# Two token blocks by turns through the first five weight slices of layer 0, with partial sums put aside

## The chip, the cores and the metric

The kernel runs on one core of one Trainium2 chip. Five engines have instruction queues of their own: TensorE (PE in the profile, PEld its weight loads), VectorE (DVE), ScalarE (ACT), GpSimd (POOL) and SyncE (SP), which here only issues DMAs. The metric is the device time of one execution in microseconds. Before the change it is 1027.12 us, the median of three runs (1025.68 to 1028.23).

## The reference, cut to what matters

```python
# linear attention with a decay per channel: batch 4, 8 heads, 768 tokens, head size 48
for t in range(S):
    cur = u * k_t (outer) v_t
    y[:, :, t] = r_t @ (state + cur)
    state = w * state + k_t (outer) v_t
x = y.transpose(0, 2, 1, 3).reshape(3072, 384)
def layer(x, w_gate, w_val, w_out):           # 384 -> 1536 -> 384
    return silu(x @ w_gate) * (x @ w_val) @ w_out
x = layer(x, moe weights)
x = layer(x / rms(x) * rms_g, moe2 weights)   # rms over the 384 of one token
```

Weights, inputs and outputs are float64 on the caller's side. The kernel gets the doubles' bits, and reads r, k, v as it needs them.

## The kernel before, in words

The 3072 tokens are eight token blocks of 384 (one half of the sequence of one batch). A pass of one block through one layer is a pair J = (layer, block). The hidden size of 1536 is cut into twelve slices of 128 (f = 0 to 11). One step of the kernel is one slice of one pass: nine matmuls for the gate (`pg`), nine for the value (`pv`), both L852, then silu (ACT, `sl`, L974), the product (DVE, `sl`, L984), a split of the product into two f16 parts (ACT `hh` L988, POOL `hl` L992), and nine matmuls that add to the output sums (`po`, L862). The nine are three products of f16 parts, for three pieces each. The output sums of a pass stay in three PSUM banks po0 to po2 over all twelve steps. At the end of a pass `evacuate` (L878, L880) takes them out; for layer 0, squares, the inverse rms on POOL (L897 to L904), scaling and a transposition (L916) follow, and the block goes to DRAM until layer 1 takes it up.

The order of passes is `ORD`: (0,0), (0,1), (0,2), (1,0), (0,3), (1,1) and so on: layer 0 leads by three. Step t is slice t % 12 of pass t // 12, so block 0 of layer 0 has steps 0 to 11, block 1 steps 12 to 23, block 2 steps 24 to 35, and layer 1 begins at step 36.

Two other kinds of work run beside the steps.

Weights: each slice arrives as doubles (`raw`, DMAs L770 to L772), and is decoded: two passes on ACT that check magnitudes (`w_abs` L799, `w_check` L804), three on DVE that put the bits together (`w_bits`, L817, L819, L821), one on ACT for the high f16 part (`w_hi`, L838) and one on DVE for the low part (`w_lo`, L842). A step needs its slice decoded. The twelve slices of layer 0 are all decoded once and kept, then layer 1's.

Attention: a block's x comes from four units of two heads each. Block 0's four units (`Unit`) work with chunks of 128 tokens: k and r are loaded (L361) into `first`, transposed (L377), weighted with tables on DVE and POOL (G: L385, F: L388), multiplied on PE (L399 to L462), with a carried state (`st` L441, `carry` L446, `sbd` L451), and give `xh` (ACT L475) and `xl` (DVE L479). Units from 4 on work with chunks of 64: transposes and weighting on DVE (L666, L514), products on POOL (L528, L529, L537, L543), states `pd` (PE L682), the carried part (ACT L609), a scan (DVE L614), the scaled states `sb` (ACT L688), `pa` (PE L676, DVE L591), and `py` (PE L566). Unit n's `pd` comes after unit n-1's `py`. Units 4 to 7 make block 1, units 8 to 11 block 2. The tables for chunks of 64 are built on POOL by `split_tables` (L725 to L735), and units from 4 on wait for them, for the end of the first four units and for three buffers that POOL clears (L718).

The order of instructions in every engine's queue is fixed when the program is built. A planner (`Plan`) gets jobs with an engine, an estimated cost and what must come before; it walks through its own estimate of time, and each time gives the engine that is free first a job that is ready, that with the longest way to the end first among those ready within 0.3 us. An engine then does its jobs in that order, whatever their real times. `due` spreads the ends of a block's units over the steps ahead of its first step, as hints for that order. DMAs from SP are a queue of the same kind ("D").

Three lines carry the order of steps before:

```python
    at_step = {J: i * NF for i, J in enumerate(ORD)}
        J, f = ORD[t // NF], t % NF
            free = [("e",) + ORD[t // NF - 1] + (g,) for g in range(NG)]
```

Of the kernel before, what the change touches and what calls it, by code (L numbers as in the profile page):

```python
# [18 lines left out]
P = 128  # L19
# [5 lines left out]
AB = 7  # L25
# [10 lines left out]
LEAD = 3  # L36
C2 = 64
# [102 lines left out]
def fast_path(ctx, tc, r, k, v, w, u, wg1, wv1, wo1, wg2, wv2, wo2, rms_g, out):  # L140
# [193 lines left out]
    class Unit:  # L334
# [385 lines left out]
    def split_tables():  # L720

        g = nc.gpsimd
        for t, x, y, reps in ((F2, E, pw[:, :, 0:8], 1), (G2, iE, ipw, 2)):
            xs = l_tile([P, HP, 8], f"xs{reps}")
            g.tensor_scalar(out=xs, in0=x[:, :, 4:12], scalar1=2.0**AB, scalar2=None, op0=ALU.mult)  # L725
            for hp in range(HP):
                for i in range(reps):
                    g.tensor_mul(
                        t[:, hp, C2 * i : C2 * i + C2].rearrange("p (a b) -> p a b", b=8),
                        xs[:, hp].unsqueeze(2).to_broadcast([P, 8, 8]), y[:, hp].unsqueeze(1).to_broadcast([P, 8, 8]))  # L730
        for j in range(2):
# [3 lines left out]
        g.tensor_scalar(out=w_carry, in0=p2[:, 1], scalar1=2.0**AB, scalar2=None, op0=ALU.mult)  # L735
# [303 lines left out]
    xts, acc, post = {}, {}, {}  # L1039
# [7 lines left out]
    at_step = {J: i * NF for i, J in enumerate(ORD)}  # L1047
# [17 lines left out]
    def last(what, J):  # L1065
        return [(what, at_step[J] + NF - 1)] if J in at_step else []
# [12 lines left out]
    add("rmsg", "D", 0.5, [("lr", HP - 1)], setup_loads2)  # L1079
    add("bonus", "D", 0.95, [("lr", HP - 1)], setup_loads3)  # L1080
# [4 lines left out]
    add("ws0", "G", 0.4, ["c1"], lambda: nc.gpsimd.memset(wscan, 0.0))  # L1085
    add("wok", "V", 0.4, ["tables", ("xl", NU1 - 1)], decay_range)

    def due(j, i):

        if not j:  # L1090
            return []
        lo, hi = at_step[0, j - 1], at_step[0, j]
        return [("g", lo + (hi - lo) * (i + 1) // HP - 1)]


    for un in units[:NU1]:
# [20 lines left out]
        add(("cy", n), "A", 0.25, [("st", n), "tables2"], lambda un=un: un.hand_on())  # L1117
        add(("sbd", n), "A", 0.82, [("st", n), "c1"] + prior("y", 2), lambda un=un: un.states2())
# [10 lines left out]
    add("tables2", "G", 4.5, ["tables", "c1"], split_tables)  # L1129
# [3 lines left out]
    for un in units[NU1:NU2]:  # L1133
# [7 lines left out]
        job_("lk", "D", 1.8, [("lr", NU1 - 1)] + p("tk", 2) + p("lr"), lambda un=un: un.load(0))  # L1141
# [76 lines left out]
    def w_jobs(q, scale, wcost, ready, ahead):  # L1218
# [4 lines left out]
        add(("abs",) + q, "A", 0.19 + 0.96 * scale, [("w",) + q] + step("chk", prev) + (held(q) if q[0] else []), lambda: w_abs(q))  # L1223
# [4 lines left out]
        add(("hi",) + q, "A", 0.19 + 0.9 * scale, [("b", 3) + q] + ([("chk",) + q] if q[0] else held(q)), lambda: w_hi(q))  # L1228
# [13 lines left out]
    def held(q):  # L1242

        tag = f"{'uv'[q[0]]}{q[1] // 2}"
        return [x for p_ in lay if RAW_AT[p_[0]][p_[1]] == tag and (p_ < q[:2] or not q[0]) for x in used(p_)]

    seq = lay + [(1, f, n) for f in range(NWH, NF) for n in "gvo"]
    for i, q in enumerate(seq):
# [4 lines left out]
        ready = [("lr", HP - 1)] + ([("w", 0, NF - 1)] if q[0] else [])  # L1253
# [8 lines left out]
    for j in range(NBLK):  # L1262
        add(("lx", j), "D", 2.1, [("put", j), ("chk", 0, NF - 1)] + ([("xl2", j - 1), ("vl2", j - 1)] if j else []),
# [15 lines left out]
    for t in range(2 * NT):  # L1279
        J, f = ORD[t // NF], t % NF  # L1280
# [198 lines left out]
```

## Time and profile before

| | |
|---|---|
| median of the runs | 1027.12 us (1025.68 to 1028.23) |
| the profiled execution | 1029.09 us, its span 1027.4 us |
| mean granted TensorE clock | 0.976 |
| PE busy | 980.6 us (95%), 7903 matmuls |
| DVE busy | 523.4 us (51%) |
| ACT busy | 519.5 us (51%) |
| POOL busy | 436.8 us (43%) |
| DMA | 76.87 MB, mean 75 GB/s |

Shares over the whole span mix a beginning, in which all engines and the DMA work at once, with a long stretch in which PE is busy nearly all of the time. How an engine stands in one stretch is read from the lines by slices and from tables of stretches. In the timeline a row has the start, the length, the engine, the code line, the operation, tiles and shapes, the count, and in brackets the idle time ahead of it with what ended it.

### The profile page before, as it was taken

The numbers are of one execution on the slowest core, as the hardware profiler recorded it, in microseconds if no ns is written. First come the engines' busy times: TensorE is split into PE (matmuls) and PEld (weight loads), VectorE is DVE, ScalarE is ACT, GpSimd is POOL, SyncE is SP. The second block draws the span as 40 slices with busy tenths as digits, with TensorE's granted clock in tenths as the row PEclk, the third lists the DMA queues.
The fourth block names the chain that finished last, engine by engine and source line by source line (L and its number), as shares of the span: only waits on it lengthen the run. The fifth ranks groups of instructions, "written<-read, shape, count | busy, mean of one in ns | idle before, by whom it ended". The sixth has DMA issues, their size and how long they took to land.

```text
span 1027.4 us, 19923 instructions
## 1 busy us (share of the span) xinstructions
PE 980.6 (95%) x7903; PEld 612.8 (60%) x7903; DVE 523.4 (51%) x817; ACT 519.5 (51%) x1121; POOL 436.8 (43%) x489
## 2 busy tenths in 40 slices
PE   6887898989999999999999999999999999999996
PEld 3655665646666666666666666666666666666663
DVE  6889997997634434474443534464332412131211
ACT  1987755865644745474455635465453524342322
POOL 9255474444353435544455335544343223321121
PEclk7889998999999999999999999999999999999998
DMA  7988765647441312331122311321010100200000
GB/s 179 226 217 208 219 185 121 169 125 125 108 47 35 84 41 46 58 94 42 33 34 51 83 41 41 64 60 41 2 24 2 54 1 3 53 24 1 24 1 27
DMA packets 152741, 76.87 MB, mean 75 GB/s; under 512 B 115648, under 2 KB 141248, under 8 KB 152640
## 3 DMA queue, kind: packets, MB, share of 16 engines
q1 hardware_dynamic: 152256, 74.93, 30.7%
q8 instruction: 64, 1.05, 0.5%
q0 software_dynamic: 384, 0.59, 0.3%
q14 instruction: 37, 0.30, 0.1%
HBM read 66.03 MB, written 9.45 MB: 73 GB/s over the span
## 4 chain that ended last, share of the span: by engine, by line
PE 70%; DVE 7%; POOL 6%; ACT 6%; issue 4%; DMA 4%; SPq 2%; DVEq 0%; POOLq 0%; ACTq 0%
PE pv L852 22%; PE pg L852 22%; PE po L862 22%; PE py L566 3%; ACT sb L630 2%; POOL hl L992 2%; POOL ap L524 2%; DMA raw<-in_moe_w_out_dram 1%; PE pd L577 1%; DVE st L614 1%; SPq L361 1%; DVE fi L819 1%; DVE fi L821 1%; ACT hh L988 1%; DVE w L842 1%
## 5 line engine op out<-in xcount | busy, mean ns | idle before, releaser
L852 PEld LDWEIGHTS <-w 128*128 128x128 f16 x3456 | 336.4, 99 | 237.4 <-issue 22.3
L992 POOL TENSOR_TENSOR hl<-sl,hh 128x384 f16<-128x384 f32 x191 | 188.2, 986 | 472.4 <-ACT hh L988 465.9
L862 PE MATMUL po<-w,hh 128*128 128x384 f16 x1152 | 282.8, 328 | 1.3 <-ACT xo L878 1.3
L988 ACT ACTIVATE hh<-sl 128x384 f16<-128x384 f32 x192 | 100.0, 521 | 339.9 <-DVE sl L982 194.8
L862 PE MATMUL po<-w,hl 128*128 128x384 f16 x576 | 189.0, 328 | 7.8 <-POOL hl L992 7.7
L982 DVE SCALAR_TENSOR_TENSOR sl<-sl,pv 128x384 f32<-128x384 f32 x96 | 53.1, 554 | 236.0 <-PE pv L852 203.0
L852 PE MATMUL pg<-xh,w 128*128 128x384 f16 x576 | 159.0, 331 | 12.1 <-DVE sl L984 9.6
L852 PE MATMUL pv<-xh,w 128*128 128x384 f16 x576 | 159.4, 332 | 0.0
L862 PEld LDWEIGHTS <-hh 128*128 128x128 f16 x1152 | 111.9, 98 | 74.4 <-issue 2.5
L852 PE MATMUL pv<-x2v,w 128*128 128x384 f16 x864 | 156.2, 326 | 0.0
L852 PE MATMUL pg<-x2g,w 128*128 128x384 f16 x864 | 156.1, 326 | 0.0
L984 DVE TENSOR_TENSOR sl<-sl,pv 128x384 f32<-128x384 f32 x96 | 52.7, 550 | 121.4 <-PE pv L852 117.3
L974 ACT ACTIVATE sl<-pg 128x384 f32<-128x384 f32 x192 | 93.3, 486 | 28.9 <-PE pg L852 27.9
L852 PE MATMUL pg<-xl,w 128*128 128x384 f16 x288 | 95.4, 331 | 1.3 <-DVE xl L479 1.3
L852 PE MATMUL pv<-xl,w 128*128 128x384 f16 x288 | 95.6, 332 | 0.0
L862 PEld LDWEIGHTS <-hl 128*128 128x128 f16 x576 | 56.6, 98 | 47.4 <-POOL hl L992 9.6
L614 DVE TENSOR_TENSOR_SCAN st<-wscan,pd 128x288 f32<-128x288 f32 x28 | 21.0, 750 | 45.6 <-ACT pd L609 26.1
L566 PE MATMUL py<-rp,sb 128*128 128x64 f16 (+1 forms) x400 | 39.3, 212 | 0.4 <-ACT sb L688 0.4
L842 DVE SCALAR_TENSOR_TENSOR w<-fi,w 128x1152 f16<-128x1152 f32 (+1 forms) x30 | 36.6, 1229 | 1.3 <-ACT w L838 1.3
L838 ACT ACTIVATE w<-fi 128x1152 f16<-128x1152 f32 (+1 forms) x30 | 28.8, 963 | 13.0 <-DVE fi L821 12.9
L475 ACT ACTIVATE xh<-py 96x384 f16<-96x384 f32 (+1 forms) x42 | 20.2, 482 | 27.9 <-PE py L566 27.6
L819 DVE SCALAR_TENSOR_TENSOR fi<-raw,fi 128x1152 int32<-128x1152 int32 x21 | 32.4, 1544 | 0.4
(209 smaller groups left out, 1190.2 us busy)
## 6 DMA issues: line engine op xcount, KB each, us to landing
raw<-in_moe_w_out_dram SPq DMA_DIRECT2D x21, 384.0 KB, 5.4
kts<-in_k_dram SPq DMA_DIRECT2D x112, 70.0 KB, 2.8
rts<-in_r_dram SPq DMA_DIRECT2D x112, 70.0 KB, 2.0
xs_d<-tt SPq DMA_DIRECT2D x32, 144.0 KB, 3.8
xt<-xs_d SPq DMA_DIRECT2D x32, 144.0 KB, 3.1
nk<-in_k_dram SPq DMA_DIRECT2D x56, 72.0 KB, 2.7
nr<-in_r_dram SPq DMA_DIRECT2D x56, 72.0 KB, 2.5
out_dram<-xo SPq DMA_DIRECT2D x7, 576.0 KB, 2.9
```

Source lines behind the costliest of these rows:

```text
L566: nc.tensor.matmul(out, a, x, start=i == 0, stop=i == len(pairs) - 1)
L614: nc.vector.tensor_tensor_scan(st, wscan, self.pd, 0.0, ALU.mult, ALU.add)
L819: vec.scalar_tensor_tensor(out=fis[q], in0=high, scalar=-0x40000000, in1=fis[q], op0=ALU.bitwise_and, op1=ALU.bitwise_or)
L838: nc.scalar.activation(out=w_parts(q)[0], in_=fis[q].bitcast(F32), func=AF.Copy, scale=2.0**WS)
L842: nc.vector.scalar_tensor_tensor(out=lo, in0=fis.pop(q).bitcast(F32), scalar=2.0**WS, in1=hi, op0=ALU.mult, op1=ALU.subtract)
L852: nc.tensor.matmul(pt, a[:, kt, :], x[:, kt, :], start=i == 0, stop=i == last)
L862: nc.tensor.matmul(po[g], a[:, sl], x, start=f == 0 and i == 0, stop=f == NF - 1 and i == 2)
L974: nc.scalar.activation(out=sl, in_=job[t]["g"], func=AF.Silu, scale=2.0 ** -(WS + (X2S if J[0] else X1S)))
L982: nc.vector.scalar_tensor_tensor(out=sl, in0=sl, scalar=2.0 ** (H2S - WS - V2S), in1=job[t]["v"], op0=ALU.mult, op1=ALU.mult)
L984: nc.vector.tensor_mul(sl, sl, job[t]["v"])
L988: nc.scalar.activation(out=job[t]["h"][0], in_=job[t]["sl"], func=AF.Copy)
L992: (nc.vector if t == 2 * NT - 1 else nc.gpsimd).tensor_sub(hl, job[t]["sl"], hh)
```

## The change

Six things are changed. The names are those of the planner's jobs.

1. Passes (0,0) and (0,1) are each cut in two at slice 5 (`CUT`). The steps are: slices 0 to 4 of block 0 (steps 0 to 4), slices 0 to 4 of block 1 (5 to 9), slices 5 to 11 of block 0 (10 to 16), slices 5 to 11 of block 1 (17 to 23). From step 24 on the order is as before. Block 1's x is due from step 5 on, block 2's spread over steps 17 to 24.
2. After slice 4 of each, `put_aside` takes the three output sums out of PSUM into an SBUF tile (one on DVE, two on ACT); at the end of the pass DVE adds it to the second part's sums (three `scalar_tensor_tensor` in place of an ACT or DVE copy).
3. The loads of r of the first four units are issued by ScalarE's queue, those of k by SyncE's. The weights' loads wait for the last k only.
4. `tables2` (`split_tables`) and the clearing of `wscan` come after the last product of the first four units on POOL. Its last line, `w_carry`, becomes a job of DVE.
5. `carry` and `sbd` of the first four units are made by DVE, not ACT.
6. The magnitudes of layer 0's weights are kept where the high part goes, not in a buffer of their own; so `w_hi` waits for `w_check`. The buffers "xt" and "tt" hold the partial sums meanwhile. The first load of a layer 1 block waits for the evacuation of block 1.

```diff
+CUT = 5
-        def load_rows(self, t, src):
+        def load_rows(self, t, src, eng=nc.sync):
...
-                    nc.sync.dma_start(out=t[q : q + 32, 0:RUN],
+                    eng.dma_start(out=t[q : q + 32, 0:RUN],
...
-            nc.scalar.activation(out=carry[self.hp], in_=self.st[:, NC], func=AF.Copy, scale=w_carry[:, self.hp : self.hp + 1])
+            nc.vector.tensor_scalar(out=carry[self.hp], in0=self.st[:, NC], scalar1=w_carry[:, self.hp : self.hp + 1], scalar2=None,
+                                    op0=ALU.mult)
...
-                nc.scalar.activation(out=sbd[self.par][q, :, D * j : D * j + D], in_=self.st[q, 0:NC], func=AF.Copy,
-                                     scale=w128(self.hp)[q])
+                nc.vector.tensor_scalar(out=sbd[self.par][q, :, D * j : D * j + D], in0=self.st[q, 0:NC], scalar1=w128(self.hp)[q],
+                                        scalar2=None, op0=ALU.mult)
...
+        mags[q] = w_parts(q)[0].bitcast(BF16)
...
+    def put_aside(J, g):
+        if J not in aside:
+            aside[J] = xi.tile([P, NG, DM], F32, tag=("tt", "xt")[J[1]], name="aside")
+        scale = 2.0 ** -(X1S + 2 * WS)
+        if g:
+            nc.scalar.activation(out=aside[J][:, g], in_=acc[J][g], func=AF.Copy, scale=scale)
+        else:
+            nc.vector.tensor_scalar(out=aside[J][:, g], in0=acc[J][g], scalar1=scale, scalar2=None, op0=ALU.mult)
...
+        if J in aside:
+            nc.vector.scalar_tensor_tensor(out=xo, in0=po, scalar=scale, in1=aside[J][:, g], op0=ALU.mult, op1=ALU.add)
...
+    SEG = [((0, j), *fs) for fs in ((0, CUT), (CUT, NF)) for j in range(2)] + [(J, 0, NF) for J in ORD[2:]]
+    STEPS = [(J, f) for J, f0, f1 in SEG for f in range(f0, f1)]
+    at_step = {J: STEPS.index((J, 0)) for J in ORD}
+    end_step = {J: STEPS.index((J, NF - 1)) for J in ORD}
...
-        lo, hi = at_step[0, j - 1], at_step[0, j]
+        lo, hi = max(at_step[0, j - 1], end_step[0, j - 2] + 1 if j > 1 else 0), at_step[0, j]
...
-        add(("lr", n), "D", 1.8, [("lk", n)], lambda un=un: un.load(1))
+        add(("lr", n), "A", 1.8, [("at", n)] + ([("lr", i - 1)] if i else ["table"]), lambda un=un: un.load(1, nc.scalar), lat=4.0)
...
-    add("tables2", "G", 4.5, ["tables", "c1"], split_tables)
+    add("w_carry", "V", 0.1, ["tables"], carry_scale)
+    add("tables2", "G", 4.5, ["tables", "c1", ("rk", HP - 1)], split_tables)
...
-        add(("hi",) + q, "A", 0.19 + 0.9 * scale, [("b", 3) + q] + ([("chk",) + q] if q[0] else held(q)), lambda: w_hi(q))
+        add(("hi",) + q, "A", 0.19 + 0.9 * scale, [("b", 3) + q, ("chk",) + q], lambda: w_hi(q))
...
-        if f:
+        if f > f0:
             free = [("o", t - 1)]
         elif t:
-            free = [("e",) + ORD[t // NF - 1] + (g,) for g in range(NG)]
+            free = [(("e" if SEG[at - 1][2] == NF else "pe"),) + SEG[at - 1][0] + (g,) for g in range(NG)]
...
+    for J, f0, f1 in SEG:
+        if f1 < NF:
+            for g in range(NG):
+                add(("pe",) + J + (g,), "A" if g else "V", 0.58, [("o", STEPS.index((J, f1 - 1)))], lambda J=J, g=g: put_aside(J, g))
```

## Rows read from the trace of the kernel before

**Rows 1.** The page: PE's busy tenths in 40 slices of the span

```profile
PE   6887898989999999999999999999999999999996
```

**Rows 2.** Stretches: length, busy us of PE, PEld, DVE, ACT, POOL, clock, DMA share, GB/s

```profile
46.37:134.73 88.36, 74.14 (x603) 47.46 (x603) 81.00 (x94) 66.70 (x108) 45.55 (x36) 0.90 0.81 218
134.73:208.84 74.11, 70.08 (x582) 45.16 (x580) 67.51 (x79) 49.65 (x91) 42.09 (x41) 0.95 0.60 150
```

**Rows 3.** PE's timeline: first gate matmuls of steps 12, 24, 36 and 39

```profile
134.73 0.33 PE L852 MATMUL pg<-xh,w 128*128 128x384 f16 x1
...
208.84 0.33 PE L852 MATMUL pg<-xh,w 128*128 128x384 f16 x1
...
274.36 0.81 PE L852 MATMUL pg<-x2g,w 128*128 128x384 f16 x4
...
287.52 0.65 PE L852 MATMUL pg<-x2g,w 128*128 128x384 f16 x3
```

**Rows 4.** Groups by line, 46.37 to 134.73 us: busy us, mean ns, idle before

```profile
L842 DVE SCALAR_TENSOR_TENSOR w<-fi,w 128x1152 f16<-128x1152 f32 x11 | 17.1, 1554 | 1.3 <-ACT w L838 1.3
...
L819 DVE SCALAR_TENSOR_TENSOR fi<-raw,fi 128x1152 int32<-128x1152 int32 x9 | 14.7, 1638 | 0.1
L821 DVE SCALAR_TENSOR_TENSOR fi<-raw,fi 128x1152 int32<-128x1152 int32 x10 | 14.1, 1408 | 0.0
...
L817 DVE TENSOR_SCALAR fi<-raw 128x1152 int32<-128x1152 int32 x9 | 7.3, 808 | 0.0
...
L984 DVE TENSOR_TENSOR sl<-sl,pv 128x384 f32<-128x384 f32 x11 | 5.9, 541 | 0.0
```

**Rows 5.** PE's timeline: py of units 4, 5 and 6, and pd of unit 5

```profile
73.55 0.30 PE L566 MATMUL py<-af,vb 128*96 128x64 f32 x2
...
75.66 0.79 PE L682 MATMUL pd<-nv,ep 64*64 64x48 f32 x20
...
80.92 0.30 PE L566 MATMUL py<-ap,nv 128*96 128x64 f32 x2
...
105.50 0.30 PE L566 MATMUL py<-af,vb 128*96 128x64 f32 x2
```

**Rows 6.** Timelines of DVE and ACT: unit 5's scan and states, unit 7's x

```profile
76.76 0.74 DVE L614 TENSOR_TENSOR_SCAN st<-wscan,pd 128x288 f32<-128x288 f32 x1
...
77.53 1.67 ACT L688 ACTIVATE sb<-st,p 64x288 f32<-64x288 f32 x2 [0.83 <-DVE st L614]
...
124.19 1.47 ACT L475 ACTIVATE xh<-py 32x384 f16<-32x384 f32 x3
...
126.66 1.69 DVE L479 SCALAR_TENSOR_TENSOR xl<-py,xh 32x384 f16<-32x384 f32 x3
```

**Rows 7.** Timelines of DVE, POOL and PE: around the first product with F

```profile
10.95 0.38 DVE L306 TENSOR_TENSOR F<-E,pw 128x128 f32<-128x128 f32 x1
...
10.19 0.31 POOL L725 TENSOR_SCALAR xs<-E 128x32 f32<-128x32 f32 x1
...
15.68 1.00 POOL L388 TENSOR_TENSOR first<-first,F 128x384 f32<-128x384 f32 x1
...
16.73 2.24 PE L420 MATMUL att<-first 64*128 64x128 f32 x12 [7.78 <-POOL first L388]
```

**Rows 8.** SP's timeline: first load of weights; then two stretches

```profile
17.64 0.42 SPq L770 DMA_DIRECT2D raw<-in_moe_w_gate_dram x1
...
10.00:20.00 10.00, 3.27 (x18) 3.04 (x18) 9.50 (x19) 0.00 (x0) 9.53 (x27) 0.64 0.72 174
20.00:30.00 10.00, 9.41 (x70) 7.20 (x70) 4.44 (x14) 6.37 (x19) 6.01 (x7) 0.67 0.99 240
```

**Rows 9.** PE's timeline: three waits, the last at step 7

```profile
157.13 0.50 PE L862 MATMUL po<-w,hl 128*128 128x384 f16 x1 [3.56 <-POOL hl L992]
...
220.55 0.48 PE L862 MATMUL po<-w,hh 128*128 128x384 f16 x2 [1.25 <-ACT xo L878]
...
100.89 0.32 PE L852 MATMUL pg<-xh,w 128*128 128x384 f16 x1 [3.00 <-DVE sl L984]
```

More of the change, by code (lines that the diff above doesn't have):

```diff
@@ L854, in in_mm, with out_mm @@
         return pt
-    def out_mm(h, w_, f, po):
+    def out_mm(h, w_, po, first, last):
         hh, hl = h
@@ L861, in out_mm @@
             for i, (a, x) in enumerate(((hh, wh), (hh, wl), (hl, wh))):
-                nc.tensor.matmul(po[g], a[:, sl], x, start=f == 0 and i == 0, stop=f == NF - 1 and i == 2)
+                nc.tensor.matmul(po[g], a[:, sl], x, start=first and i == 0, stop=last and i == 2)
     def on_act(layer, blk):
-        return () if (layer, blk) == (1, NBLK - 1) else (1,) if layer else (0, 1)
+        return () if (layer, blk) in ((0, 0), (0, 1), (1, NBLK - 1)) else (1,) if layer else (0, 1)
+    def put_aside(J, g):
[6 more added lines that the diff above has]
+            nc.vector.tensor_scalar(out=aside[J][:, g], in0=acc[J][g], scalar1=scale, scalar2=None, op0=ALU.mult)
     def evacuate(layer, blk, g):
@@ L992, in step_hl, with step_o @@
         (nc.vector if t == 2 * NT - 1 else nc.gpsimd).tensor_sub(hl, job[t]["sl"], hh)
-    def step_o(t, f, q, J):
-        if f == 0:
+    def step_o(t, q, J, first, last):
+        if first:
             acc[J] = [ps.tile([P, DM], F32, tag=f"po{g}", name=f"po{g}") for g in range(NG)]
-        out_mm(job.pop(t)["h"], W[q + ("o",)], f, acc[J])
+        out_mm(job.pop(t)["h"], W[q + ("o",)], acc[J], first, last)
     def check_range():
@@ L1065, in last @@
     def last(what, J):
-        return [(what, at_step[J] + NF - 1)] if J in at_step else []
+        return [(what, end_step[J])] if J in end_step else []
     add("wu", "D", 1.9, [], load_tables)
@@ L1222, in w_jobs @@
         add(("w",) + q, "D", wcost, ready, (lambda: w_load(*q)) if len(q) == 2 else (lambda: w_load2(q[1], q[2])))
-        add(("abs",) + q, "A", 0.19 + 0.96 * scale, [("w",) + q] + step("chk", prev) + (held(q) if q[0] else []), lambda: w_abs(q))
+        add(("abs",) + q, "A", 0.19 + 0.96 * scale, [("w",) + q] + step("chk", prev) + held(q), lambda: w_abs(q))
         add(("chk",) + q, "A", 0.28 + 0.96 * scale, [("abs",) + q, "c1"], lambda: w_check(q))
@@ L1244, in held @@
         tag = f"{'uv'[q[0]]}{q[1] // 2}"
-        return [x for p_ in lay if RAW_AT[p_[0]][p_[1]] == tag and (p_ < q[:2] or not q[0]) for x in used(p_)]
+        return [x for p_ in lay if RAW_AT[p_[0]][p_[1]] == tag and p_ < q[:2] for x in used(p_)]
     seq = lay + [(1, f, n) for f in range(NWH, NF) for n in "gvo"]
@@ L1252, in fast_path @@
             continue
-        ready = [("lr", HP - 1)] + ([("w", 0, NF - 1)] if q[0] else [])
+        ready = [("lk", HP - 1)] + ([("w", 0, NF - 1)] if q[0] else [])
         tag = RAW_AT[q[0]][q[1]]
@@ L1262, in fast_path @@
     for j in range(NBLK):
-        add(("lx", j), "D", 2.1, [("put", j), ("chk", 0, NF - 1)] + ([("xl2", j - 1), ("vl2", j - 1)] if j else []),
+        add(("lx", j), "D", 2.1, [("put", j)] + [("e", 0, 1, g) for g in range(NG)] + ([("xl2", j - 1), ("vl2", j - 1)] if j else []),
             lambda j=j: post.__setitem__(("xt", j), load_x2(j)))
@@ L1279, in fast_path @@
     for t in range(2 * NT):
-        J, f = ORD[t // NF], t % NF
+        J, f = STEPS[t]
+        J0, f0, f1 = next(x for x in SEG if x[0] == J and x[1] <= f < x[2])
+        at = SEG.index((J0, f0, f1))
         layer, blk = J
```

37 lines of the change are left out of this document (17 added, 20 removed).

## The prediction

> **What bounds the kernel now.** I read the page's lines by slices first: PE is at nine tenths or more from the eighth slice of 25.7 us on, and not before [rows 1]. So time can be won only in the first 200 us or so, or by fewer matmuls, and the change takes none away. The table of stretches says how much is there. From the first step at 46.37 to step 12 at 134.73 PE idles 88.36 - 74.14 = 14.2 us, and its granted clock is 0.90; from there to step 24 it idles 4.0 us at a clock of 0.95 [rows 2, 3]. In the first stretch DVE is busy 81.00 of 88.36 us, 92%: it, not PE, sets the pace. Steps 36 to 39, with nothing in their way, start (287.52 - 274.36) / 3 = 4.39 us apart [rows 3], while one slice's decoding takes 1.554 + 1.638 + 1.408 + 0.808 = 5.41 us of DVE [rows 4]. Twelve steps on twelve fresh slices therefore run at DVE's pace, and attention for block 1 lies on the same engine. Steps 12 to 23 need no new slices and run near PE's.
>
> The change turns this round: ten steps use five slices. The other side is that block 1's x, ready before step 12, is now needed for step 5. So the end hangs on one time, T5, at which step 5 can start. From step 24 on both kernels do the same, PE-bound; I count the difference at step 24's start, 208.84 before.
>
> **From step 5 to step 24.** The stretch before from step 12 to step 24 has twelve steps, the matmuls of four units and the stalls of one block's end, in 74.11 us [rows 2]. Now there are seven steps more, 7 x 4.39 = 30.7, so 104.8. Two terms are added. The sums have to leave PSUM after step 9: the wait for that before was 1.25 (ACT's evacuation) [rows 9], I take it. After step 4 the same lies inside the wait for T5. And PE will have idled ahead of step 5, after which its clock falls: at step 7 it waited 3.00 [rows 9], and the 18 matmuls from 100.89 to 105.50 [rows 5] took 4.61, against 2/3 x 4.39 = 2.93 at full pace, so 1.7 more. Step 24 starts at T5 + 104.8 + 1.25 + 1.7 = T5 + 107.8. The change pays when T5 is under 101.0.
>
> The stall at a block's end, 3.56 for `hl` behind the inverse rms on POOL [rows 9], stays and is in the 74.11; it moves to steps 16 and 17. Three additions on DVE at the end of two passes stand in place of copies, 3 x 0.54 each, by L984 [rows 4]: between nothing and 3.2 us for both; PE has a gate and a value group to do meanwhile, I take nothing. In front of them in DVE's queue may be a decoding step of up to 1.64.
>
> **The start.** `tables2` begins on POOL at 10.19 and holds the first product with F until 15.68, while F itself is written by 10.95 + 0.38 = 11.33; PE sits idle 7.78 for that product [rows 7]. With the tables behind, it can start at 11.33: 4.35 us sooner, and the first four units with it, if nothing else is late. Next in line are r and k of the later units. Between nothing and 4.35, I take 4.35, since r's loads come sooner too: SP issues its first load of weights at 17.64, after 32 loads of k and r [rows 8], half of which now go by ACT, idle until then (0.00 busy from 10 to 20). The tables are wanted only by unit 4. That cover is the four units on POOL; if unit 4's weighting comes first, up to 5 us of tables lie ahead of it.
>
> What the weights gain by this is bounded. DMA is at 0.72 from 10 to 20 and at 0.99 from 20 to 30 [rows 8]: only the free share of the first, 2.8 us, can be used. By the times of issue alone they would come 7.4 us sooner, half of 14.9. The Trainium skill ("DMA: Bandwidth & Descriptors", Issuing engines are not separate DMA queues) says that DMAs from several engines run on the same 16 DMA engines and that a second issuer saves only issue time. By that rule it is 2.8, by two independent queues 7.4; the 0.99 is with the rule. DVE could use the time, busy only 4.44 from 20 to 30.
>
> `carry` and `sbd` on DVE are three small operations per unit, for which the nearest DVE row is 0.54 for 384 elements: nothing to 6.5 us for four units, I take 3.2, as these have 144 and 48. ACT gains what it loses nowhere on the path. That `w_hi` waits for the check costs ACT's queue nothing new but order; ACT is at 66.70 of 88.36 us [rows 2]. Later loading of layer 1's blocks has until step 36.
>
> **T5 from the units' chain.** Unit 4's `py` starts at 73.55 [rows 5], so at 69.2 with the start's gain. From unit 5's `pd` at 75.66 to its scan at 76.76 is 1.10, to `sb` at 77.53 0.77, `sb` itself 1.67, and `py` lasts 75.66 - 73.55 = 2.11: 5.65 a unit is the floor when all follows at once [rows 5, 6]. Units 4 and 5 were 7.37 apart, as PE did a value group first. With units 6 and 7 wanted, I take 6.2, a third of the way: their stages are now the most urgent jobs, but steps 3 and 4 share PE. Unit 7's `py` starts at 69.2 + 3 x 6.2 = 87.8, and `py` 2.11, `xh` 1.47 and `xl` 1.69 [rows 6] give **T5 = 93.1** (91.4 at the floor, 96.6 at 7.37).
>
> **T5 from DVE's work.** By 134.73 DVE had done all before step 12. Now slices 5 to 11 and six products can wait: 7 x 5.41 + 6 x 0.54 = 41.1 us of work, at 92% busy 44.8 us. 134.73 - 44.8 - 4.35 (start) + 3.5 (3.2 for the new operations at 92%) = 89.1. The chain is later, so it decides. After T5 DVE has five steps, 22 us, for about four slices ahead of step 10, then a slice per 4.39 with a lead; the seven slices, 37.9 us, are done well before step 16, and block 2's units before step 24.
>
> **The sum.** Step 24 at 93.1 + 107.8 = 200.9, 7.9 us sooner. The profiled execution took 1029.09 (its span 1027.4), 1.97 over the median of 1027.12. So 1021.2 for it, and **1019.2** against the median.
>
> **Rivals.**
> - Early x: units and decoding interleave so well that the chain's floor is reached from an earlier unit 4, and DVE's sum decides. T5 = 89.1, less 2.8 where sooner weights fill its idle time: 86.3. Step 24 at 194.1, 14.7 sooner, **1012.4**. For it: DVE idled only 8% and could be given the right order. Against: the stages alternate between four engines, each with a fixed queue. By full independence of the two DMA queues it would be 81.7, 4.6 better still.
> - The start isn't sooner: loads of units 1 to 3 or the check ahead of `w_hi` hold the first four units. T5 = 97.4, 3.6 sooner, **1023.5**. Against it stands the 7.78 of PE for one product.
> - Slower: weight slices stay ahead of the units. DVE's order comes from estimates, and between `py` of units 5 and 6 lay 24.6 us before [rows 5]. If each of units 5 to 7 finds one slice, 5.41, ahead of it in DVE's queue, T5 = 93.1 + 16.2 = 109.3, step 24 at 217.1, 8.3 later: **1035.4**. From one and a half such slices on the change loses. Against: step 5 now hangs on these units and the later slices on nothing before step 10, so the planner ranks them lower; but it gives an idle engine whatever is ready.
>
> That the change doesn't do what it says could be only in its order; the steps' order on PE is held by the PSUM banks.
>
> **How the numbers follow.** Chances: 0.43 for the forecast (T5 from 90 to 101), 0.24 for early x, 0.16 for no sooner start, 0.17 for slices ahead. A measurement of this kernel can tell 0.3%, 3.1 us, from no change: T5 up to 97.9 is faster, 97.9 to 104.1 the same. Faster: 0.38 of the forecast, all of early x, 0.05 of the third: 0.67. The same: 0.05, 0.11 and 0.01: 0.17. Slower: 0.16. The range goes from 1007 (T5 = 81.7 with nearly all of the new DVE operations free) to 1029 (T5 = 103, a good half of the slices' price), and leaves out about 0.14 above and 0.05 below. The likeliest case alone has 1016 to 1024.
>
> **What would show it.** Right: gate matmuls of step 5 (block 1, slice 0) start at 91 to 97, just after the last `xl` of unit 7; step 24's near 201; the first product with F near 11.3; `py` of units 4 to 7 some 6 us apart; `put_aside` with PE idle under 1.5 after step 9. Wrong: step 5 held by weights or by the sums in PSUM; slices 5 and later decoded on DVE ahead of units 6 and 7; a long PE wait between steps 10 and 24; or step 36 held by layer 1's decoding, pushed later by what was moved ahead.

## The result, and the profile after

The changed kernel takes **1040.8 us** (median of 4 runs, 1038.65 to 1044.55), the kernel before 1027.67 beside it: ratio 1.0112 [1.0087, 1.0138], 1.1% slower. The forecast was 1019.2. The profiled execution took 1038.65, 9.56 over the one before; its span is 1037.0, 9.6 over. Lines have moved by 1 to 13: L852 is now L853, L862 L863, L566 L569, L682 L685, L676 L679, L479 L482, L817 to L842 one more, L984 L997, L770 to L772 L775 to L777.

The page's slices of TensorE (PE), which answer to [rows 1]: the second and third are weaker than before, and PE is at nine tenths from the fifth on.

```profile
PE   7568999999999999999999999999999999999996
```

PE's timeline at the starts of steps 5, 24 and 36 (start, us, engine, line, operation):

```profile
106.73 0.33 PE L853 MATMUL pg<-xh,w 128*128 128x384 f16 x1
...
215.40 0.33 PE L853 MATMUL pg<-xh,w 128*128 128x384 f16 x1
...
281.88 0.81 PE L853 MATMUL pg<-x2g,w 128*128 128x384 f16 x4
```

T5, at which step 5 starts, is 106.73, not 93.1. Step 24 is 6.6 us later than before, step 36 7.5 [rows 3], and the end 9.6. The table of stretches, from step 0 (48.13) to 5, 5 to 24 and 24 to 36, with two of the start (columns as in [rows 2]):

```profile
10.00:20.00 10.00, 6.90 (x38) 5.29 (x39) 8.64 (x22) 2.36 (x7) 7.20 (x10) 0.61 0.72 166
20.00:30.00 10.00, 8.40 (x73) 7.36 (x71) 3.81 (x10) 2.36 (x7) 6.59 (x13) 0.84 0.83 206
48.13:106.73 58.60, 42.47 (x390) 28.60 (x390) 50.03 (x60) 35.57 (x57) 24.45 (x22) 0.81 0.83 199
106.73:215.40 108.67, 101.30 (x795) 63.88 (x793) 104.07 (x115) 75.04 (x133) 64.75 (x52) 0.98 0.58 153
215.40:281.88 66.48, 62.58 (x461) 39.12 (x460) 58.71 (x87) 40.94 (x92) 31.01 (x32) 0.97 0.58 137
```

In steps 0 to 4 PE idles 16 us at a clock of 0.81, and VectorE (DVE) is busy only 50.03 of 58.60, 85%, where the forecast took 92% [rows 2] (before, over its steps 0 to 4 alone, it was 33.79 of 39.31, 86%). So DVE, which was to set the pace, itself waits. The timelines of GpSimd (POOL), SyncE (SP), DVE, ScalarE (ACT) and PE around the start show for what (the bracket is the idle time before, and what ended it):

```profile
11.22 1.24 POOL L390 TENSOR_TENSOR first<-first,F 128x384 f32<-128x384 f32 x1 [1.14 <-DVE F L308]
```
```profile
23.04 0.43 SPq L775 DMA_DIRECT2D raw<-in_moe_w_gate_dram  x1
...
61.33 1.28 SPq L658 DMA_DIRECT2D vb<-in_v_dram  x2
```
```profile
30.76 0.78 DVE L818 TENSOR_SCALAR fi<-raw 128x1152 int32<-128x1152 int32 x1 [4.92 <-DMA kts<-in_k_dram]
```
```profile
30.74 1.25 ACT L800 ACTIVATE w<-raw 128x1152 bf16<-128x1152 f32 x1 [5.53 <-DMA kts<-in_k_dram]
```
```profile
32.89 0.88 PE L428 MATMUL att<-vb,kg 128*64 128x48 f32 x12 [4.49 <-ACT kg L407]
...
48.13 0.50 PE L853 MATMUL pg<-xh,w 128*128 128x384 f16 x1 [4.67 <-ACT w L839]
```

The first product with F starts at 11.22, as forecast (11.33; before 15.68, [rows 7]). But slice 0's weights are first issued at 23.04, 5.4 us later than before [rows 8], since unit 4's k, u, natural k and r, and r now stand ahead of them in SP's queue. DVE and ACT have slice 0's decoding in their fixed order ahead of operations of the first four units. Both stand still for it until 30.7 (a DMA ended the wait; `kts` is only the profile's name for it, the operation reads `raw`), and PE waits 4.49 for ACT's `kg`, which stands behind. The start's 4.4 us are gone: block 0's x is complete at 49.7, against 49.1.

The list of PE's waits up to step 24 (total us, times, longest), then PE's timeline of the second block's units:

```profile
PE pg L853 <- DVE w L843: 6.7, 2, 4.7
PE pg L853 <- ACT w L839: 5.1, 2, 4.7
PE att L428 <- ACT kg L407: 5.1, 2, 4.5
PE pd L685 <- DMA vb<-in_v_dram: 4.0, 3, 3.0
...
PE po L863 <- DVE aside L877: 2.0, 1, 2.0
PE pd L685 <- DMA nv<-in_v_dram: 1.8, 2, 1.2
```
```profile
72.94 0.47 PE L569 MATMUL py<-af,vb 128*96 128x64 f32 x2
...
78.78 0.35 PE L569 MATMUL py<-ap,nv 128*96 128x64 f32 x2 [0.84 <-DVE ap L594]
...
87.27 0.30 PE L569 MATMUL py<-af,vb 128*96 128x64 f32 x2
...
97.41 0.30 PE L569 MATMUL py<-ap,nv 128*96 128x64 f32 x2
```

`py` of units 4 to 7 comes 5.8, 8.5 and 10.1 us apart. The v of unit 4 was issued only at 61.33, behind slices 1 to 6. At the end DVE's timeline has two decoding operations of slice 5, first wanted at step 10, ahead of unit 7's last `xl`; slice 5 decoded ahead of unit 7 was one of the forecast's signs of being wrong:

```profile
99.96 2.06 DVE L820 SCALAR_TENSOR_TENSOR fi<-raw,fi 128x1152 int32<-128x1152 int32 x1
102.06 2.05 DVE L822 SCALAR_TENSOR_TENSOR fi<-raw,fi 128x1152 int32<-128x1152 int32 x1
104.14 1.69 DVE L482 SCALAR_TENSOR_TENSOR xl<-py,xh 32x384 f16<-32x384 f32 x3
```

### The profile page after: what moved, and what is told of

It is laid out like the page before. It is cut to its first block, busy times and chain, and to the rows that moved or that the text cites. A ratio compares the mean times of both kernels' runs of the same rounds, so it can differ in the third digit from the quotient of the medians.

```text
span 1037.0 us, 19913 instructions
## 1 busy us (share of the span) xinstructions
PE 981.6 (95%) x7903; PEld 614.4 (59%) x7903; DVE 536.4 (52%) x836; ACT 514.6 (50%) x1109; POOL 441.1 (43%) x488
## 4 chain that ended last, share of the span: by engine, by line
PE 66%; DMA 8%; DVE 8%; ACT 5%; POOL 5%; SPq 4%; issue 3%; DVEq 0%; POOLq 0%; ACTq 0%
PE pg L853 20%; PE po L863 20%; PE pv L853 20%; DMA raw<-in_moe_w_out_dram 3%; PE py L569 3%; POOL ap L527 2%; ACT sb L633 2%; DVE fi L818 1%; DVE fi L820 1%; PE pd L580 1%; POOL hl L1005 1%; DMA first<-in_k_dram 1%; DVE fi L822 1%; DVE st L617 1%; SPq L504 1%
## 5 line engine op out<-in xcount | busy, mean ns | idle before, releaser
L853 PEld LDWEIGHTS <-w 128*128 128x128 f16 x3456 | 335.5, 98 | 237.3 <-issue 8.2
L863 PE MATMUL po<-w,hh 128*128 128x384 f16 x1152 | 281.1, 326 | 3.5 <-DVE aside L877 2.0
L863 PE MATMUL po<-w,hl 128*128 128x384 f16 x576 | 187.8, 326 | 4.9 <-POOL hl L1005 4.7
L853 PE MATMUL pg<-xh,w 128*128 128x384 f16 x576 | 159.8, 333 | 13.2 <-DVE w L843 6.7
L853 PE MATMUL pv<-xh,w 128*128 128x384 f16 x576 | 158.5, 330 | 0.0
L863 PEld LDWEIGHTS <-hh 128*128 128x128 f16 x1152 | 111.6, 98 | 76.4 <-issue 4.2
L853 PE MATMUL pv<-x2v,w 128*128 128x384 f16 x864 | 156.2, 326 | 0.0
L853 PE MATMUL pg<-x2g,w 128*128 128x384 f16 x864 | 156.1, 326 | 0.0
L997 DVE TENSOR_TENSOR sl<-sl,pv 128x384 f32<-128x384 f32 x96 | 52.7, 549 | 111.7 <-PE pv L853 111.4
L853 PE MATMUL pg<-xl,w 128*128 128x384 f16 x288 | 95.7, 332 | 0.0
L853 PE MATMUL pv<-xl,w 128*128 128x384 f16 x288 | 95.1, 330 | 0.0
L863 PEld LDWEIGHTS <-hl 128*128 128x128 f16 x576 | 56.3, 98 | 44.4 <-POOL hl L1005 7.1
L617 DVE TENSOR_TENSOR_SCAN st<-wscan,pd 128x288 f32<-128x288 f32 x28 | 21.1, 752 | 49.9 <-ACT pd L612 29.0
L569 PE MATMUL py<-rp,sb 128*128 128x64 f16 (+1 forms) x400 | 40.1, 214 | 1.8 <-ACT sb L691 1.6
L843 DVE SCALAR_TENSOR_TENSOR w<-fi,w 128x1152 f16<-128x1152 f32 (+1 forms) x30 | 38.7, 1297 | 1.8 <-ACT w L839 1.7
L531 POOL TENSOR_TENSOR rk<-nr,nk 128x288 f32<-128x288 f32 x28 | 34.5, 1232 | 2.3 <-DVE gd L536 1.7
```

The lines of the kernel that those rows point to most:

```text
L531: nc.gpsimd.tensor_mul(rk, self.nr, self.nk)
L569: nc.tensor.matmul(out, a, x, start=i == 0, stop=i == len(pairs) - 1)
L617: nc.vector.tensor_tensor_scan(st, wscan, self.pd, 0.0, ALU.mult, ALU.add)
L843: nc.vector.scalar_tensor_tensor(out=lo, in0=fis.pop(q).bitcast(F32), scalar=2.0**WS, in1=hi, op0=ALU.mult, op1=ALU.subtract)
L853: nc.tensor.matmul(pt, a[:, kt, :], x[:, kt, :], start=i == 0, stop=i == last)
L863: nc.tensor.matmul(po[g], a[:, sl], x, start=first and i == 0, stop=last and i == 2)
```

## Experiments

Theory A: the loss is in the written orders. They follow from load times that the planner takes too short, so engines wait in place. The planner gives SP's queue 1.8 us for the k of one of the first units and 4.1 for a slice of weights. In SP's timeline the k of the four units takes 12.68, 3.17 each, and slices 3 to 6 begin 5.4 to 6.2 us apart:

```profile
2.26 12.68 SPq L363 DMA_DIRECT2D first<-in_k_dram  x16
...
39.02 0.31 SPq L775 DMA_DIRECT2D raw<-in_moe_w_gate_dram  x1
...
44.64 0.31 SPq L775 DMA_DIRECT2D raw<-in_moe_w_gate_dram  x1
```

Rivals: the turns cost by themselves, whatever the order (T); DVE's work holds step 5 (E); the edits of the start do harm (B). The expectations bring in further letters, C, D, F and G, each told there. The table has all runs, with times from their traces (idle is PE's, from step 0 to 5 with the wait ahead of step 0, and from step 24 to 50; ratios are to runs of before on the same chip):

| run | median | ratio, 95% | step 0 | step 5 | step 24 | step 36 | idle 0–5 | idle 24–50 |
|---|---|---|---|---|---|---|---|---|
| before | 1027.67 | 1 | 46.4 | 85.7 (block 0) | 208.8 | 274.4 | 9.3 | 3.6 |
| after | 1040.8 | 1.0112 [1.0087, 1.0138] | 48.1 | 106.7 | 215.4 | 281.9 | 20.8 | 5.8 |
| e1 | 1031.41 | 1.0021 [1.0003, 1.0038] | 41.5 | 88.0 (block 0) | 208.7 | 273.1 | 16.4 | 3.5 |
| e2 | 1044.9 | 1.0158 [1.0141, 1.0175] | 47.2 | 109.7 | 220.6 | 293.5 | 20.4 | 7.3 |
| e3 | 1037.8 | 1.0092 [1.0061, 1.0123] | 42.5 | 103.5 | 213.0 | 283.6 | 18.1 | 7.7 |
| e4 | 1044.77 | 1.0145 [1.0119, 1.0172] | 47.1 | 111.6 | 219.6 | 291.9 | 21.3 | 7.0 |
| e5 | 1041.03 | 1.0109 [1.0092, 1.0126] | 46.3 | 113.0 | 222.2 | 288.4 | 20.5 | 5.0 |
| e6 | 1036.58 | 1.0067 [1.0044, 1.0089] | 44.2 | 103.1 | 208.3 | 276.3 | 14.8 | 8.8 |
| e7 | 1036.77 | 1.0082 [1.0059, 1.0105] | 45.0 | step 8: 114.4 | 212.8 | 280.3 | 13.9 | 3.7 |
| e8 | 1041.99 | 1.0109 [1.0066, 1.0152] | 49.9 | 109.2 | 214.2 | 283.9 | 18.3 | 8.4 |
| e9 | 1029.87 | 1.0007 [0.9982, 1.0033] | 40.2 | 97.9 | 198.9 | 259.1 | 17.7 | 9.1 |
| e10 | 1031.09 | 1.0020 [0.9999, 1.0041] | 41.0 | 84.2 (block 0) | 205.9 | 275.3 | 13.3 | 7.6 |
| e11 | 1034.67 | 1.0055 [1.0035, 1.0075] | 41.2 | 104.8 | 207.0 | 272.6 | 21.7 | 7.8 |
| e12 | 1031.2 | 1.0029 [1.0013, 1.0045] | 40.4 | step 8: 114.5 | 200.0 | 270.5 | 14.2 | 11.3 |
| e13 | 1031.52 | 1.0019 [1.0001, 1.0036] | 40.5 | 100.9 | 199.8 | 275.8 | 17.1 | 11.4 |
| e14 | 1031.62 | 1.0020 [1.0004, 1.0036] | 41.1 | 83.9 (block 0) | 205.5 | 272.3 | 14.2 | 5.7 |
| e15 | 1025.94 | 0.9966 [0.9951, 0.9982] | 40.9 | 97.9 | 196.2 | 270.5 | 15.0 | 11.3 |

At steps 24 and 50 PE has the same matmuls behind it in all of them (1413 and 2387, but for one record that some traces lack). At step 36 it has 1873, but 1814 in e9 and 1849 in e12, which do some of block 3's attention later: their step 36 can't be set beside the others'.

**e1: whole passes, the start's edits kept** (layer 1's loads wait as before the change).

```
-    SEG = [((0, j), *fs) for fs in ((0, CUT), (CUT, NF)) for j in range(2)] + [(J, 0, NF) for J in ORD[2:]]
+    SEG = [(J, 0, NF) for J in ORD]
...
-  (layer, blk) in ((0, 0), (0, 1), (1, NBLK - 1))
+  (layer, blk) == (1, NBLK - 1)
```

> Whole passes again (twelve slices of block 0, then of block 1); all else of the change stays (r by ACT's queue, tables later, states on DVE, magnitudes in place). Theory A (the loss comes from the order of loads that the turns bring about: unit 4's loads ahead of slice 0's, unit 4's v behind slices 1 to 6): the first step starts at 42 to 45 and the time is 1021 to 1026, about 4 below the kernel before. Rival B (the edits of the start are what costs): first step at 48 or later, time 1030 or more.

Step 0 starts 4.9 us sooner than before, at 41.5, so the start's edits do what the forecast gave them; B had step 0 at 48 or later. By step 2 it is gone (63.0, before 56.5): in this order the first slices don't follow. Without turns the loss of 1.1% shrinks to 0.2%. The time is in B's range and not in A's (1021 to 1026): the edits of the start don't cost much, but win nothing.

**e2: the turns alone** (r on SP, tables early, states on ACT again).

```
-  add(("lr", n), "A", 1.8, ... lambda un=un: un.load(1, nc.scalar), lat=4.0)
+  add(("lr", n), "D", 1.8, [("lk", n)], lambda un=un: un.load(1, nc.sync))
...
-  nc.vector.tensor_scalar(out=carry[self.hp], ...)
+  nc.scalar.activation(out=carry[self.hp], ...)
```

> Turns and put_aside with magnitudes in place, but r's loads on SP, tables early and the first units' states on ACT, as before the change. Theory A: slow as the changed kernel or a little slower, 1038 to 1048, since unit 4's loads stand ahead of slice 0 here too. Rival B: 1015 to 1025, as the turns then gain and nothing at the start is lost.

As A expected and not B (1015 to 1025), and slower than all parts together: in these orders the turns carry the whole loss.

**e3: only r's loads back on SP** (the first edit of e2 alone).

> The changed kernel with r's loads back on SP between k's, all else as changed. Theory A: 1038 to 1046, slice 0 lands some 2 to 4 us later still, first step at 49 to 52. Rival C (the planner counts ACT's loads as a second DMA and so puts slice 0's first operations too early on DVE and ACT; with one queue they come at their time): DVE's 4.9 us and ACT's 5.5 us of waiting for slice 0 go, first step at 45 to 47, 1034 to 1038.

Step 0 comes at 42.5: A's 49 to 52 is missed, and C holds for the start. SP's 32 loads now take 15.8 us, 1.97 for a unit's k or r, near the planner's 1.8; with r on a second queue k took 3.17. But step 5 comes only at 103.5. The start's wait is gone and a new one stands in its place, 9.72 us for unit 4's v, in PE's timeline:

```profile
59.14 1.29 PE L685 MATMUL pd<-vb,ef 64*64 64x48 f32 x19 [9.72 <-DMA vb<-in_v_dram]
```

**e4: unit 4's loads only after slice 1's.**

```
-  job_("lk", "D", 1.8, [("lk", NU1 - 1)] + p("tk", 2) ...
+  job_("lk", "D", 1.8, [("lk", NU1 - 1), ("w", 0, 1)] + p("tk", 2) ...
```

> The changed kernel, but unit 4's loads may go only after slice 1's (the order of the queue comes out as slice 0, then unit 4's k, u, nk, nr, r, then slice 1). Theory A: slice 0 lands near 25 in place of 30.8, the wait of DVE and ACT for it goes, the first step starts at 43 to 46; but unit 4's v still stands behind slice 7, so step 5 only comes 0 to 4 us sooner than 106.7: 1035 to 1041. Rival D (the place of v does not matter, T5 follows from the first step's time): step 5 some 4 us sooner and all of it kept, 1035 to 1037.

**e5: v of units 4 to 7 by POOL's queue.**

```
+  eng = nc.gpsimd if self.n < 2 * HP else nc.sync
...
-  nc.sync.dma_start(
+  eng.dma_start(
```

> The changed kernel, but the v of units 4 to 7 is loaded by POOL's queue, so that unit 4's v no longer stands behind slices 1 to 6 in SP's. Theory A (places in the load queue set T5): unit 4's py starts at 62 to 67 in place of 72.9 and step 5 at 96 to 101: 1031 to 1036. Rival E (DVE's work up to T5 sets it, whoever comes first): unit 4's py is sooner, but step 5 stays at 103 to 107, 1038 to 1042.

Both miss: step 5 is 5 to 6 us later than in the changed kernel, outside every expectation. Each edit takes its own wait away and the rewritten order has others: in e4 PE waits 12.0 us for unit 4's v, in e5 DVE 5.3 us for a load of keys and PE 6.9 for `af`. Moving single loads doesn't mend an order.

**e6: the planner's time for a slice's load 5.9 in place of 4.1** (and `xh2` waits for the gains, which that order needs).

```
-  w_jobs(q, 1.0, 4.1, ready, ahead)
+  w_jobs(q, 1.0, 5.9, ready, ahead)
```

> The changed kernel with only the planner's estimate of a slice's load raised from 4.1 to 5.9 us (nearer to the 5.3 to 6 us that SP's rows show); only orders change, and unit 4's v comes behind slice 4 in the queue, not slice 6. Theory A: fewer operations wait in a fixed place for a load, step 5 at 97 to 102, 1031 to 1037. Rival E: step 5 stays at 103 to 107, 1038 to 1042.

Nothing but orders differ, and 4 us of the loss are gone, as A expected; step 5 at 103.1 is later than A's 97 to 102.

**e7: the cut after slice 7** in place of 4: `CUT = 8`.

> The changed kernel with the cut at slice 8 in place of 5: block 1's x is wanted for step 8. In the order of loads slice 0 is ahead of unit 4's loads again. Theory A (a cut at 5 wants block 1's x before slices can be kept flowing): DVE fills the units' waits with slices, step 8 starts at 106 to 112 and step 24 at 203 to 209: 1023 to 1030. Rival F (any cut costs, by the sums put aside and the later work pushed back): 1033 or more.

Some 4 us back too, but the time is F's, not A's, and step 8 starts at 114.4, later than A's 106 to 112; PE idles 13.9 from step 0 to 5 and 6.3 from 5 to 12 (1.4 in the changed kernel).

**e8: less decoding, same order.** The third decoding operation of layer 0 runs on one eighth of its columns, so the lowest three bits of the other weights are left out.

```
+  m = w_size(q) // 8 if q[0] == 0 else w_size(q)
-  vec.scalar_tensor_tensor(out=fis[q], in0=low, ...)
+  vec.scalar_tensor_tensor(out=fis[q][:, :m], in0=low[:, :m], ...)
```

> The changed kernel with the third decoding operation of layer 0's slices on an eighth of the columns (the lowest three bits of most of layer 0's weights are left out); the order is unchanged. That takes some 1.3 us per slice off DVE, 6 to 8 us by step 5. Rival E (DVE's work sets T5): step 5 at 99 to 101, 1032 to 1036. Theory A (DVE waits in its fixed order anyway): step 5 moves by less than 3 us, 1038 to 1041.

L822 takes a mean of 562 ns in place of 1606, about 1.0 us less of DVE per slice. E expected step 5 at 99 to 101; it starts at 109.2, no sooner than in the changed kernel (106.7). DVE waits longer in its places instead: 6.67 us in place of 4.92 for slice 0, 3.5 in place of 1.0 for a load of r. In this order DVE's work does not set T5; rival E falls for the changed kernel.

**e9: all load times as measured** (e6, and:)

```
-  add(("lk", n), "D", 1.8 ...    add(("lr", n), "A", 1.8 ...
+  add(("lk", n), "D", 3.1 ...    add(("lr", n), "A", 3.1 ...
-  job_("lk", "D", 1.8 ... "lr" 1.8 ... "n" + w_ 0.9 ... "nv" 0.9
+  job_("lk", "D", 2.4 ... "lr" 2.4 ... "n" + w_ 1.3 ... "nv" 2.0
```

> The turns stay; only the durations that the planner gives to loads are raised to what the traces show (a slice of weights 5.9 us, keys and queries of the first units 3.1 each, of later units 2.4, natural keys and queries 1.3, values 2.0), so only the written orders differ. Theory A (orders written from load times that are too short make DVE, ScalarE and GpSimd wait in place, and this costs the turns their gain): step 5 starts by 100 us, TensorE idles under 13 us in steps 0 to 5, time 1020 to 1028. Rival T (the turns cost by themselves: four units in a row, some 8 us each, can't be hidden behind ten half passes, whatever the order): step 5 at 103 or later, idle in steps 0 to 5 at 15 or more, time 1034 to 1042.

The loss is gone: 1029.87, ratio 1.0007. Step 5 starts at 97.9. The time lies between A's and T's ranges, and the idle time, 17.7, is T's. The stretches of the start and from step 0 to 5, then DVE's waits from 20 to 110 us:

```profile
20.00:30.00 10.00, 10.00 (x108) 9.48 (x106) 8.49 (x24) 5.70 (x16) 8.09 (x18) 1.00 0.70 192
...
40.20:97.90 57.70, 44.04 (x399) 30.01 (x400) 49.65 (x60) 32.33 (x53) 22.82 (x20) 0.82 0.74 187
```
```profile
DVE xl L482 <- ACT xh L478: 7.5, 4, 2.7
DVE st L443 <- PE po L428: 0.6, 1, 0.6
DVE st L617 <- ACT pd L612: 0.4, 1, 0.4
```

DVE no longer waits for a DMA (in the changed kernel 5.9 us, 4.9 of it for slice 0), and PE is busy 10.00 of the 10 us from 20 on. Unit 4's loads still stand ahead of slice 0's, whose first issue is at 23.50; only the decoding now stands behind the first units. So the harm was the place in DVE's and ACT's orders, not the load's. But from step 0 to 5 it still takes 57.7 us (58.6 in the changed kernel), and of the 9.9 us won on before at step 24 3.0 are left at step 50, 2.7 at the end of the spans, and nothing by the medians (the profiled execution is 3.5 us under its kernel's median): PE idles 7.1 from step 36 to 50, longest for the turned r of unit 13:

```profile
268.82 1.24 PE L679 MATMUL pa<-rp,kp 64*64 64x64 f32 x24 [4.24 <-DVE rp L517]
```

**e10: e9's times with e1's whole passes.**

> The same raised durations, but whole passes in place of the turns (scales back on ScalarE, block 1's tiles not needed early). Theory A: without turns the order matters less; 1026 to 1032, not better than the kernel with turns and raised durations. Rival T: the turns are what costs, so this is 6 to 12 us under the kernel with turns and raised durations, 1022 to 1031, with step 24 by 208 us.

1031.09 and 1029.87 can't be told apart: with fitting orders the turns neither cost nor win. T falls as the cause, and so does A's hope that they would win. The raised times do nothing without turns either (e1 1.0021, e10 1.0020): short load times cost only together with the turns. Step 2 comes at 52.2 here, so with a fitting order the first slices do follow.

**e11: e6 with e3's edit.**

> Turns with the slice's load put at 5.9 us, and the first queries back on SyncE's queue. If the two gains found singly (4 us from each) come from different waits, they add: step 5 at 98 to 100, 1030 to 1033. If both only moved the same waits for the second block's units, no more than one of them is left: step 5 at 102 to 104, 1035 to 1038.

1034.67, in between; the start gains, step 5 doesn't (104.8). Step 0 comes at 41.2 with all of the first loads on SP, so the start's gain needs no second queue.

**e12: e9's times with the cut after slice 7.**

> Turns with the raised durations and the cut after slice 7 in place of 4, so that block 1's tiles are needed three slices later. If the units' chain sets where the second block can start (rival T), a later cut gives it 3 half passes of some 4 us to hide behind: step 8 by 108 us, 1024 to 1032, below the cut at 5 with the same durations. If the slices set the pace of the first pass (as without turns), it idles for slices 5 to 7 as before the change: 1032 to 1038.

Not better than the cut at 5 (1.0029 against 1.0007), and step 8 comes at 114.5, not by 108. Step 24 comes at 200.0, near e9's: that too is given back, with 11.3 us idle from step 24 to 50.

**e13: e9, but layer 1's slices at the old 4.1.**

```
-  w_jobs(q, 1.0, 5.9, ready, ahead)
+  w_jobs(q, 1.0, 4.1 if q[0] else 5.9, ready, ahead)
```

> As e9 (turns, raised load durations), but layer 1's slices keep the planner's old 4.1 us. Theory A (a load put ahead of what is needed sooner costs its wait): up to step 24 as e9 (step 5 at 97 to 99, step 24 at 198 to 200); the wait of TensorE for the turned r of the 64-token unit in steps 36 to 50 falls from 4.2 to under 1.5 us, and time is 1022 to 1027. Rival G (given back whatever the order, by DVE's work for layer 1 that has no other place): idle in steps 24 to 50 stays at 8 to 11 us, 1028 to 1032.

The wait for the turned r stays (4.13), now before step 36; my explanation by the place of layer 1's loads falls, and rival G's numbers are met or nearly so (1031.5 us, 11.4 us idle). Of these 11.4 PE waits 4.1 for the turned r and 5.6 for POOL's `hl` (before: nothing and 2.3). A line of PE's waits from 199.8 to 346.4, SP's and DVE's timelines and the stretch up to step 36:

```profile
PE po L863 <- POOL hl L1005: 5.6, 3, 4.0
```
```profile
243.46 2.00 SPq L363 DMA_DIRECT2D rts<-in_r_dram  x4
```
```profile
259.68 0.81 DVE L669 STREAM_TRANSPOSE rp<-rts 128x384 f32<-128x384 f32 x1
...
261.26 0.53 DVE L517 TENSOR_TENSOR rp<-rp,F 128x384 f32<-128x384 f32 x1
```
```profile
226.60:275.80 49.20, 43.32 (x308) 27.68 (x307) 46.16 (x56) 31.56 (x63) 22.76 (x19) 0.93 0.47 120
```

r's loads were issued by 245.5, and DVE came to it at 259.68: it is busy 46.16 of 49.20 us, 94%, mostly with layer 1's decoding. So this wait is DVE's; the three for `hl` were not followed up. A sooner step 24 brings PE sooner to places where it waits for DVE and POOL.

**e14: e13's times with whole passes.**

> The same durations as e13, whole passes in place of turns. If the turns are worth something once orders fit, this is 3 to 8 us above e13. If they are worth nothing, the two are within 3 us.

Equal again (1.0020 and 1.0019), within the 3 us: the second pair that says the turns are worth nothing.

**e15: e13 with e8's shortened operation** (the same bits left out).

> As e13, with the third decoding operation of layer 0's slices on one eighth of its columns (the lowest three bits of the other weights are left out): 1.2 us less of DVE per slice, orders unchanged. If DVE's work holds step 5 now (it is busy 67.2 of the 77.9 us up to it in e9): 4 to 6 us sooner than in e13, 92 to 95. If waits and the units' chain hold it, as in e8: within 2 us of e13.

Step 5 is 3.0 us sooner than in e13, between the two expectations. That alone says little: e9 has e13's order on every engine up to 170 us and all of the decoding, and its step 5 starts at 97.9 too. The stretch from 92 to 98 us in e9, then in e13, shows why:

```profile
92.00:98.00 6.00, 5.36 (x45) 4.05 (x44) 3.24 (x5) 4.73 (x9) 0.01 (x1) 1.00 1.09 262
...
92.00:98.00 6.00, 5.44 (x29) 4.47 (x29) 1.82 (x2) 3.05 (x7) 0.00 (x0) 0.50 1.09 257
```

PE's granted clock is 1.00 (2.4 GHz) in e9 and 0.50 (1.2 GHz) in e13, after idle times of 2.20 and 1.66 us just before 88.2 and 88.0. So executions of one order can differ by 3 us at step 5 through PE's clock alone. DVE's rows don't have this: unit 7's scan starts at 90.55 in e9, and in e13 and in e15 at

```profile
90.39 0.75 DVE L617 TENSOR_TENSOR_SCAN st<-wscan,pd 128x288 f32<-128x288 f32 x1 [0.39 <-ACT pd L612]
...
87.26 0.75 DVE L617 TENSOR_TENSOR_SCAN st<-wscan,pd 128x288 f32<-128x288 f32 x1 [0.39 <-ACT pd L612]
```

With less decoding it is 3.1 us sooner, although slice 0's first operation started 1.0 later. From step 0 to 5 it takes 57.0 in place of 60.4, and DVE's busy time falls from 51.13 to 47.51:

```profile
40.90:97.90 57.00, 45.84 (x399) 30.31 (x400) 47.51 (x63) 34.10 (x56) 21.76 (x20) 0.82 0.79 199
```

With orders that fit, DVE's work does hold unit 7's chain, where in e8 it did not. The gain lasts to the end: 5.6 us under e13 by the medians, with all of e15's times (up to 1026.96) under all of e13's (from 1028.69). It leaves work out, so it is no version to use; no complete kernel here beats the one before.

## Why the prediction was wrong

The miss of 21.6 us is T5 13.6, the stretch to step 24 0.9, after step 24 3.0 (9.6 at the span's end less 6.6 at step 24), and 4.1 from executions: before was profiled 1.97 above its median, after 2.15 under.

- **The step that failed is T5 from the units' chain**, 93.1 against 106.73. By its terms: unit 4's `py` at 72.94, not 69.2 (+3.7); a unit each 8.16, not 6.2 (+5.9 for three); from unit 7's `py` to its last `xl` 8.4, not 5.3 (+3.1); 0.9 until step 5. Each took DVE and ACT to be free when the chain came. In the trace they weren't: slice 0's decoding held the first units, v came behind six slices, and slice 5's operations stood ahead of `xl`.
- **"The start 4.35, I take 4.35"** was right for the product (11.22) and for the edit (e1: 4.9; e11 has it without the second queue), but not in this order: step 0 at 48.1 where 46.4 - 4.35 = 42.0 was counted. I named "if nothing else is late" and didn't price the weights, whose first issue moved from 17.64 to 23.04 behind unit 4's loads. That the orders are to blame is shown by e9: load times in the planner alone bring step 0 to 40.2 and step 5 8.8 sooner.
- **The pace** from step 0 to step 5, 51.1 in the forecast (93.1 - 42.0), was 57 to 67 us in every order tried with this cut. e9 removes the waits for DMA and still takes 57.7. There the sum of DVE's work was short: 92% of 47.1 us (89.1 - 42.0) is 43.3 busy, and 49.65 were measured. One part is work that the forecast moved sooner with the start, though its weights didn't come sooner: by step 0 the four decoding operations had run 3, 3, 2 and 1 times before and 1, 1, 1 and 0 times in e9, which is 7.9 us by [rows 4]. Another is that a slice took 6.0 in e9 (1.758 + 1.591 + 1.596 + 1.090), not 5.41 [rows 4]. The parts weren't separated. That DVE's work holds unit 7 is shown by e15, for a fitting order only.
- **The rival "weight slices stay ahead of the units"** (T5 109.3, step 24 at 217.1) came nearest, and its mechanism is in the rows; it had 0.17. It was incomplete: the late start, not only slices between units.
- **Right:** step 24 is T5 + 108.67, against T5 + 107.8. The 2.02 that PE waited for `put_aside` after step 9 (1.25 taken) is in it. A later T5 thus went one to one to step 24. Luck has a part in it: with fitting orders the same nineteen steps took 101.0 (e9) and 98.9 us (e13), so 107.8 was too long for those.
- **Right in the number:** the second queue's gain was bounded at 2.8 us by DMA's free share, against 7.4 by issue: k's and r's loads ended at 14.94 instead of 17.64, 2.7 sooner. The share that rose wasn't the one named, though: from 10 to 20 us it is 0.72 as before, and in the first 10 us 0.74 in place of 0.62; in e1, where the weights follow at once, it is 0.89 from 10 to 20. The Trainium skill ("DMA: Bandwidth & Descriptors", Issuing engines are not separate DMA queues) says that DMAs of several issuing engines run on the same 16 DMA engines and interleave. The 2.7 in place of 7.4 agrees with it.
- **"From step 24 on both kernels do the same, PE-bound"** cost 3 us in the changed kernel, 2.2 of it PE's idle time from step 24 to 50, and with fitting orders most of what was won: e9 is 9.9 sooner than before at step 24 and 2.7 at the end of its span; PE's idle time from step 24 to 50 is 9.1 to 11.4 in e9, e12 and e13, 3.6 before. The reading of [rows 1] passed over a sign of this: PE isn't at nine tenths from the eighth slice on, since the ninth, 205 to 231 us, in which step 24 starts, has 8. e13's rows put the longest single wait there down to DVE, 94% busy, two thirds of it with layer 1's decoding; a larger sum, 5.6, is for POOL's `hl`. Neither was shortened to prove it, so this part is read, not shown.

So the expected gain went to two places: in the changed kernel into waits that fixed orders hold in place, and, once these are mended, into waits after step 24 for DVE and POOL.

## What to carry to other kernels

Where a planner writes the order, a change of what is urgent is first a change of every queue. Before counting a chain's gain, list what the new order can put ahead of it on each in-order engine and queue, and price one load that comes late. Raise the planner's load times to those in the trace before judging a reordering: here that alone was worth 11 us with the turns, and nothing without them. And a gain made early can be given back in the stages behind it: count it at the end, not at the first common step. Before a time within one trace is set beside that of another, look at PE's clock in both, or take rows of an engine that it doesn't touch.

## What was not expected of the hardware

A decoding operation's time depended on whether POOL worked beside it. L820 and L822 run 42 times on a whole slice in the changed kernel. The 12 that no operation of POOL overlaps take 1.34 to 1.36 us; the 30 others take 1.34 to 2.08, and every one above 1.36 is among them. So the means move with the order: L822 took 1606 ns in steps 0 to 4 of the changed kernel and L818 965, against 1408 and 808 before [rows 4]. This is read from the trace; no run changed POOL's work to prove it.

With a second queue beside it, SP stood still for transfers: the 16 loads of k took 2.26 to 14.94, 0.79 each, and SP waited 6.6 us of that for earlier loads of k to go through. In e3, with r on SP too, 32 loads took 0.49 each; a load of weights is mostly issued in 0.43 to 0.46.
